# Splitting expert weights and tokens into high and low parts: the low part handed to VectorE later, the weight halves loaded apart

## The chip, the cores and the metric

The kernel runs on one core of one Trainium2 chip. The metric is device time of one launch in microseconds. Before the change it is 754.46 us, the median of three runs (753.71 to 755.72). A difference of about 0.3%, 2.3 us here, is what a measurement of this kernel can tell from none.

## The reference

Attention over 8 batches and 8 heads (512 local positions with a window of 32 and 32 global ones, head size 64) makes 4352 tokens of 512 numbers. They go to 8 experts of 544 places each: the largest (token, expert) logits are taken first. Each expert is a feed-forward layer.

```
logits = x @ w_gate                       # x: 4352 x 512, w_gate: 512 x 8
order = np.argsort(-flat)
for idx in order:                         # greedy: expert e takes at most cap = 544 tokens
    tok, e = (int(idx) // E, int(idx) % E)
    if assigned[tok] >= 0 or counts[e] >= cap:
        continue
    assigned[tok] = e
for e in range(E):
    h = np.maximum(x[mask] @ w1[e], 0.0)  # w1[e]: 512 x 1024
    out[mask] = h @ w2[e]                 # w2[e]: 1024 x 512
```

## The kernel before

**Two stages.** The attention, its gate and the first search for an expert fill the first 278 us of the trace. The change does not touch them. Then `experts` runs eight rounds, `ffn(0)` to `ffn(7)`, one expert each.

**A round.** Products are made in a reduced float format, so each operand is split in a high part (`w1h`, `w2h`, `xh`, `hh`: a copy by ACT that rounds) and a low part (`w1l`, `w2l`, `xl`, `hl`: what is left, a subtraction on DVE). Each product is three matmuls: high by high, high by low, low by high. The first layer (L874) has 8 blocks `f` of 128 columns, each in two halves of 272 tokens; a half is 12 matmuls over the four row blocks `d` of w1, and for `d` = 2 it reads `w1h2` and `w1l2`. ACT then writes `hh` by a Relu (L876) and, after the second half, `h32` (L878); DVE writes `hl`. Then come 64 small matmuls for the last 32 tokens (L889), and 96 matmuls of the second layer (L899), 24 for each of four token tiles. A round of w1 splits has eight pieces: four with columns 0 to 511 (in the code `a`, needed from `f` = 0) and four with columns 512 to 1023 (`b`, needed from `f` = 4).

**Routing beside it.** `Routing.phase` finds the next expert and its tokens by eight search steps. Each is a chain: DVE makes `r_G`, PE multiplies it (`R<-r_oh,r_G`), DVE makes `r_ce`, PE multiplies (`R<-r_ce,big`), DVE scans (`r_pm`) and makes the next `r_G`. From the last step comes `widx` (where the next expert's weights lie), then `r_ohl`, 34 small matmuls `R<-r_ohl,rhs`, the matmuls `R<-c,r_w`, and from them `idx` (where its tokens lie). GpSimd then gathers five tiles of tokens `xg`, PE turns them (L742), ACT writes `xh` (L744) and DVE `xl`.

**What sets the order.** The code writes each engine's instructions in a fixed order, by a plan. `V.now` is the plan's clock, moved on by `step(ns)` after each matmul; `V.busy` is when DVE would be done by estimated durations, whatever DVE waits for. `todo` holds jobs with a tag, a time and a condition; `step` issues one that is due, then as much routing as the plan's clock allows. `calm()` holds splits back while DVE has 200 ns of work ahead. `force(tag)` issues what is left of a tag at once: `force(f"b{ph}")` stands before `f` = 4, `force(f"w{ph}")` (w2) before the small matmuls. `at` puts a job in `todo`. In `split`, ACT's copy is followed at once by DVE's subtraction (L718 to L720), so DVE's next instructions stand behind one that waits for ACT. `load_w1` and `load_w2` gather the two halves (1 MB each) back to back on GpSimd's queue.

Of the kernel before, what the change touches and what calls it, by code (L numbers as in the profile page):

```python
# [8 lines left out]
F32 = mybir.dt.float32  # L9
# [12 lines left out]
E = 8  # L22
# [351 lines left out]
SLACK = 100  # L374
PACE = 250
RELU = 700
CU = 64
LAND = 1000
CF = 1024
# [304 lines left out]
def experts(ctx, tc, A, xd, ident, rt, out):  # L684
# [21 lines left out]
    def load_w1(ph):  # L706
        raws = []
        for k in range(2):
            raw = st.tile([128, 2, FF], F32, name="w1r", bufs=2)
            gather(raw.rearrange("p a b -> p (a b)"), A["w1"], k * E * 128 * 2 * FF, rt.widx[ph][:, :1])  # L710
            raws.append(raw)
        return raws

    def load_w2(ph):
        for k in range(2):
            gather(w2r[k].rearrange("p a b -> p (a b)"), A["w2"], k * E * 128 * 4 * DM, rt.widx[ph][:, :1])

    def split(hi, lo, raw, eng):  # L718
        nc.scalar.activation(hi, raw, AF.Copy)  # L719
        eng.tensor_tensor(lo, raw, hi, op=ALU.subtract)  # L720

    def split_w1(raws, j, eng):
        q = slice(512 * (j % 2), 512 * (j % 2) + 512)
        split(w1h[j // 2][:, q], w1l[j // 2][:, q], raws[j // 4][:, (j // 2) % 2, q], eng)

    def split_w2(j, eng):
        split(w2h[j], w2l[j], w2r[j // 4][:, j % 4], eng)

    def load_x(ph):
        xg = []  # L730
# [4 lines left out]
            xg.append(g)  # L735
        return xg

    def trans_x(xg, t):
        n = sizes[t]
        p = ps.tile([128, 4, 128], F32, name="H", bufs=4)  # L740
        for d in range(4):
            nc.tensor.transpose(p[:, d, :n], xg[t][:n, 128 * d:128 * d + 128], ident[:n, :n])  # L742
        q = slice(128 * t, 128 * t + n)
        nc.scalar.activation(xh[:, :, q], p[:, :, :n], AF.Copy)  # L744
        V.tensor_tensor(xl[:, :, q], p[:, :, :n], xh[:, :, q], op=ALU.subtract)

    out4 = out.rearrange("n (c d) -> (n c) d", c=4)

# [9 lines left out]
    V = rt.V  # L758
    V.now = V.busy = 0.0
    pool, dma, need = [0.0], [0.0], [0.0]  # L760
    fill, todo, raw1 = [], [], {}
    done, cur, mid, wrote = [False], [0], [-1], [0.0]

    def pool_op(ns, nbytes=0):
        pool[0] = max(pool[0], V.now) + ns
        if nbytes:
            dma[0] = max(dma[0], pool[0] + 1800) + nbytes / 360.0
            return dma[0] + 300
        return pool[0]

    def calm():
        return V.busy < V.now + AHEAD

    def chain():
        for ph in range(1, E):
# [16 lines left out]
    def force(tag, n=9):  # L792
        while pending(tag) and n:
            todo.pop([x[0] for x in todo].index(tag))[3]()
            n -= 1

    def step(ns):
        V.now += ns
        low()
        for i, (tag, t, cond, f) in enumerate(todo):  # L800
            if t <= V.now and (cond is None or cond()):
                todo.pop(i)
                f()
                break
        while not done[0] and V.now >= need[0]:
            v = next(routing, None)
            if v is None:
                done[0] = True
            elif v >= 0:
                need[0] = v  # L810

    def low1(p, j):
        split_w1(raw1[p], j, V)

    def low2(j):
        split_w2(j, V)

    def get_w1(p, half):
        raw1[p] = load_w1(p)
        r = [pool_op(1040, 1 << 20) for _ in range(2)]  # L820
        for i in range(4):
            at(f"a{p}", r[i // 2], lambda j=2 * i: low1(p, j), lambda: (half or mid[0] == p - 1) and calm())
        for i in range(4):
            at(f"b{p}", r[i // 2], lambda j=2 * i + 1: low1(p, j), lambda: mid[0] == p - 1 and calm())

    def get_x(p):
        xg = load_x(p)
        for t in range(5):
            r = pool_op(1040, sizes[t] * 2048)
            at(f"x{p}", r, lambda t=t: trans_x(xg, t), lambda: mid[0] == p - 1)  # L830

    def get_w2(p):
        load_w2(p)
        r = [pool_op(1040, 1 << 20) for _ in range(2)]
        for j in range(8):
            at(f"w{p}", r[j // 4], lambda j=j: low2(j), lambda: cur[0] == p and calm())

    def out_tile(ph, t, p):
        n = sizes[t]
# [14 lines left out]
    def ffn(ph):  # L854
# [53 lines left out]
    heat = ps.tile([128, HF], F32, name="H", bufs=4)  # L908
    for _ in rt.phase(0):
        if raws is None and 0 in rt.widx:  # L910
            raws = load_w1(0)
    xg = load_x(0)
    load_w2(0)
    for _ in range(HEAT):
        nc.tensor.matmul(heat[:, :128], ident, ident, start=True, stop=True)
    raw1[0] = raws
    for _ in rt.setup(slice(0, 34)):
        pass
    for j in range(4):
        split_w1(raws, 2 * j, nc.vector)  # L920
    for t in range(5):
        trans_x(xg, t)
    V.now = V.busy
    for j in range(4):
        at("b0", 0, lambda j=j: low1(0, 2 * j + 1), calm)
# [82 lines left out]
```

## Time and profile before

| what | us |
|---|---|
| median of three runs | 754.46 |
| profiled execution: its own time | 759.57 |
| its span | 757.8 |
| PE busy | 695.0 |
| DVE busy | 505.8 |
| ACT busy | 306.9 |
| GpSimd busy | 159.9 |
| round 1, from its first matmul of layer one to the next round's | 59.92 |
| round 2 | 60.14 |
| round 3 | 60.07 |
| round 4 | 60.77 |
| round 5 | 63.01 |
| round 6 (no search beside it) | 55.13 |

Times in the trace count from the start of the span. A row of a timeline gives the start in us, the duration, engine, line, operation and what it writes and reads; in brackets stands how long the engine was idle before it and what ended that. PE is TensorE's matmuls and PEld its loads of weights. A matmul's duration counts its way through the array, and the next starts before it ends, so the pace of PE is read from the distance of the starts. Nearly all work of DVE is recorded under one line, so one goes by the tiles' names.

### The profile page before, as it was taken

The page shows a single profiled execution, that of the slowest core. Times are in us where ns is not written, and L with a number is a line of the kernel's source. Part 1 is how long each engine was busy: PE and PEld are TensorE (multiplying, and loading weights), DVE is VectorE, ACT ScalarE, POOL GpSimd, SP SyncE. Part 2 cuts the span into 40 slices and gives each one's busy share as a digit, 9 for nine tenths or more (in the row PEclk, how much of TensorE's full clock was granted, in tenths as well). Part 3 has the DMA queues.
Part 4 walks back from the last instruction along what each step waited for, and adds up shares of the span by engine and source line. Part 5 has one row for each costly group of instructions (what it writes and reads, how often), then busy time and mean ns, then how long its engine had stood idle before and what let it go on. Part 6 is the DMA issues. An engine that isn't in the chain of part 4 may idle for free. (4 is left out here: it accounts for less than half of the span.)

```text
span 757.8 us, 21849 instructions
## 1 busy us (share of the span) xinstructions
PE 695.0 (92%) x9012; PEld 569.1 (75%) x9012; DVE 505.8 (67%) x1855; ACT 306.9 (40%) x841; POOL 159.9 (21%) x190
## 2 busy tenths in 40 slices
PE   8999999999995289999999999999999997999993
PEld 6667777777773169879879878878977975988982
DVE  6787877787776778678677776767766865641400
ACT  4656766665751034243143234333324322542310
POOL 5221221221100130330231142033034034312011
PEclk9999999999997569999999999999999999999997
DMA  9998878979701160350171071062063047331000
GB/s 358 410 356 312 320 279 292 325 277 331 279 20 58 41 241 1 124 194 26 53 253 38 6 270 68 6 238 99 2 235 106 2 165 241 106 116 55 2 32 28
DMA packets 32419, 120.56 MB, mean 159 GB/s; under 512 B 6720, under 2 KB 6976, under 8 KB 24128
## 3 DMA queue, kind: packets, MB, share of 16 engines
q1 hardware_dynamic: 22080, 67.78, 24.3%
q0 software_dynamic: 10240, 51.39, 19.1%
q8 instruction: 71, 1.16, 0.6%
q14 instruction: 28, 0.23, 0.1%
HBM read 101.32 MB, written 17.83 MB: 157 GB/s over the span
## 5 line engine op out<-in xcount | busy, mean ns | idle before, releaser
L874 PE MATMUL H<-xh,w1h 128*128 128x272 f32 x512 | 151.9, 297 | 4.3 <-ACT xh L744 4.3
L874 PE MATMUL H<-xh,w1l 128*128 128x272 f32 x512 | 152.4, 298 | 0.0
L874 PE MATMUL H<-xl,w1h 128*128 128x272 f32 x512 | 151.9, 297 | 0.1
L145 ACT ACTIVATE p<-p,nm 128x128 f32<-128x128 f32 x256 | 81.8, 391 | 66.5 <-DVE ls L165 34.3
L876 ACT ACTIVATE hh<-H 128x272 fp32r<-128x272 f32 x128 | 51.0, 398 | 134.4 <-PE H L874 114.0
L899 PE MATMUL Y<-w2h,hh 128*128 128x512 f32 x256 | 103.9, 406 | 0.0
L899 PE MATMUL Y<-w2l,hh 128*128 128x512 f32 x256 | 102.0, 398 | 0.0
L874 PEld LDWEIGHTS H<-xh,w1h 128*128 128x128 f32 x512 | 98.3, 192 | 4.9 <-ACT xh L744 4.4
L899 PE MATMUL Y<-w2h,hl 128*128 128x512 f32 x256 | 101.8, 398 | 0.0
L874 PEld LDWEIGHTS H<-xl,w1h 128*128 128x128 f32 x512 | 98.2, 192 | 1.4 <-DVE xl L406 0.8
L874 PEld LDWEIGHTS H<-xh,w1l 128*128 128x128 f32 x512 | 98.0, 191 | 0.7 <-issue 0.2
L406 DVE TENSOR_TENSOR w2l<-w2r,w2h 128x512 fp32r<-128x512 f32 x64 | 43.9, 690 | 48.4 <-ACT w2h L719 47.9
L134 PE MATMUL S<-qk,qz 128*64 128x128 f32 x1024 | 70.8, 279 | 5.5 <-DVE qz L86 2.4
L86 POOL COPY qz<-q 64x544 f32<-64x544 f32 x60 | 38.3, 639 | 151.7 <-DMA q<-in_qk_dram 106.6
L134 PEld LDWEIGHTS S<-qk,qz 128*64 128x64 f32 x1024 | 55.0, 137 | 18.4 <-issue 11.3
L406 DVE SCALAR_TENSOR_TENSOR hl<-H,hh 128x272 fp32r<-128x272 f32 x128 | 54.5, 435 | 20.3 <-ACT h L878 10.7
L141 DVE CUSTOM_DVE_ANT_0 p<-S,mask 128x128 f32<-128x128 f32 x256 | 58.7, 285 | 6.2 <-PE S L134 5.1
L847 ACT ACTIVATE y<-Y 128x512 f32<-128x512 f32 x32 | 19.1, 598 | 103.0 <-PE Y L899 79.5
L719 ACT ACTIVATE w1h<-w1r 128x512 fp32r<-128x512 f32 x64 | 36.9, 624 | 55.7 <-DVE r_c L406 29.8
L406 DVE TENSOR_TENSOR w1l<-w1r,w1h 128x512 fp32r<-128x512 f32 x60 | 40.9, 686 | 26.5 <-ACT w1h L719 24.6
L899 PEld LDWEIGHTS Y<-w2h,hh 128*128 128x128 f32 x256 | 48.1, 188 | 11.4 <-issue 2.0
L899 PEld LDWEIGHTS Y<-w2h,hl 128*128 128x128 f32 x256 | 48.1, 188 | 11.1 <-issue 0.8
(166 smaller groups left out, 1169.3 us busy)
## 6 DMA issues: line engine op xcount, KB each, us to landing
vw<-in_vw_dram SPq DMA_DIRECT2D x32, 1040.0 KB, 8.1
qk<-in_qk_dram SPq DMA_DIRECT2D x32, 432.0 KB, 5.6
q<-in_qk_dram SPq DMA_DIRECT2D x32, 272.0 KB, 6.1
xd<-xs SPq DMA_DIRECT2D x8, 1024.0 KB, 6.7
xd<-xg SPq DMA_DIRECT2D x64, 8.0 KB, 6.0
xg<-xd,idx POOLq DMA_INDIRECT x40
mask<-in_mask_dram SPq DMA_DIRECT2D x1, 512.0 KB, 4.9
cf<-in_cf_dram SPq DMA_DIRECT2D x1, 512.0 KB, 12.5
```

The lines of the kernel that those rows point to most:

```text
L86: eng.tensor_copy(z[r, :, h, :], q[r].rearrange("p (j i) -> p j i", i=32))
L134: nc.tensor.matmul(st[64 * r:64 * r + 64, c, :], z[:, j].rearrange("p h i -> p (h i)"), kw[:, k0:k0 + 128], start=True, stop=True)
L141: nc.vector.tensor_tensor_reduce(s.p[:, c, :], st[:, c, :], mask[:, 4 * s.u + c, :], 1.0, -BIG, ALU.add, ALU.max, nm[:, c:c + 1])
L145: nc.scalar.activation(s.p[:, c, :], s.p[:, c, :], AF.Exp, bias=nm[:, c:c + 1], scale=SCALE)
L406: return op(*args, **kw)
L719: nc.scalar.activation(hi, raw, AF.Copy)
L847: nc.scalar.activation(y[:n], p[:n], AF.Copy)
L874: nc.tensor.matmul(p, w[d][:, fs], x[:, d, q], start=(d + k == 0), stop=(d + k == 5))
L876: nc.scalar.activation(hh[:, f, q], p, AF.Relu)
L899: nc.tensor.matmul(p, h[:, f, q], w[f], start=(f + k == 0), stop=(f + k == 9))
```

## The change

`split` issues ACT's copy alone. With `late` set, DVE's subtraction goes into a list `lag` with a time: `SPLIT` = 850 ns later on the plan's clock for weights, 1290 ns for tokens (`SPLIT + 4 * 110`). `settle` issues what is due in each `step`; `settle(True)` issues all that is left, at the end of `force` (for all tags but `out`) and at a round's end. `calm` also holds splits back while two are in `lag`. Only the first round's first splits stay as they were. The second half of w1 and of w2 is gathered by a job of its own, `APART` = 3000 ns of the plan after the first; the `b` pieces wait until both halves are loaded and the `a` pieces issued.

```
+SPLIT = 850
+APART = 3000
...
-    def split(hi, lo, raw, eng):
+    def split(hi, lo, raw, late, ns=SPLIT):
         nc.scalar.activation(hi, raw, AF.Copy)
-        eng.tensor_tensor(lo, raw, hi, op=ALU.subtract)
+
+        def rest():
+            V.tensor_tensor(lo, raw, hi, op=ALU.subtract)
+        if late:
+            lag.append((V.now + ns, rest))
+        else:
+            rest()
...
-        nc.scalar.activation(xh[:, :, q], p[:, :, :n], AF.Copy)
-        V.tensor_tensor(xl[:, :, q], p[:, :, :n], xh[:, :, q], op=ALU.subtract)
+        split(xh[:, :, q], xl[:, :, q], p[:, :, :n], late, SPLIT + 4 * 110)
...
     def calm():
-        return V.busy < V.now + AHEAD
+        return V.busy < V.now + AHEAD and len(lag) < 2
...
     def force(tag, n=9):
...
+        if tag != "out":
+            settle(True)
+
+    def settle(all=False):
+        while lag and (all or lag[0][0] <= V.now):
+            lag.pop(0)[1]()

     def step(ns):
         V.now += ns
         low()
+        settle()
...
     def get_w1(p, half):
-        raw1[p] = load_w1(p)
-        r = [pool_op(1040, 1 << 20) for _ in range(2)]
-        for i in range(4):
-            at(f"a{p}", r[i // 2], lambda j=2 * i: low1(p, j), lambda: (half or mid[0] == p - 1) and calm())
-        for i in range(4):
-            at(f"b{p}", r[i // 2], lambda j=2 * i + 1: low1(p, j), lambda: mid[0] == p - 1 and calm())
+        raw1[p] = []
+
+        def go(k):
+            raw1[p].append(load_w1(p, k))
+            r = pool_op(1040, 1 << 20)
+            for j in (4 * k, 4 * k + 2):
+                at(f"a{p}", r, lambda j=j: low1(p, j), lambda: (half or mid[0] == p - 1) and calm())
+            for j in (4 * k + 1, 4 * k + 3):
+                at(f"b{p}", r, lambda j=j: low1(p, j),
+                   lambda: mid[0] == p - 1 and not pending(f"a{p}", f"g{p}") and calm())
+        go(0)
+        at(f"g{p}", V.now + APART, lambda: go(1))
...
             out_tile(ph, t, p)
         while nxt < E and (pending(f"g{nxt}", f"h{nxt}", f"a{nxt}", f"x{nxt}", f"v{nxt}") or nxt not in raw1):
             step(120)
+        settle(True)
```

`get_w2` is cut in two by a `go(k)` of its own in the same way, and line numbers of the experts' code grow by up to 21.

**ACT, the pieces of w1 for round 3.** Before, in the second layer of round 2, ACT has the last pieces `w1h1`, `w1h2`, `w1h3` (columns 512 to 1023) ahead of the tokens `xh`; `y` is a finished output tile:

```order
L847 ACTIVATE y_7685<-Y_7586 128x512
L719 ACTIVATE w1h1_4822<-w1r_7509 128x512
L719 ACTIVATE w1h2_4823<-w1r_7511 128x512
L719 ACTIVATE w1h3_4824<-w1r_7511 128x512
L744 ACTIVATE xh_4847<-H_7723 128x4x128
L744 ACTIVATE xh_4847<-H_7734 128x4x128
```

Now, in layer one of round 3, the last two of them stand between block `f` = 3 (`hh` twice and `h32`) and block `f` = 4 (the last two `hh`):

```order
L895 ACTIVATE hh_4849<-H_7947 128x272
L895 ACTIVATE hh_4849<-H_7969 128x272
L897 ACTIVATE h32_4851<-H_7969 128x32
L717 ACTIVATE w1h2_4823<-w1r_7537 128x512
L717 ACTIVATE w1h3_4824<-w1r_7537 128x512
L895 ACTIVATE hh_4849<-H_8013 128x272
L895 ACTIVATE hh_4849<-H_8033 128x272
```

Two pieces moved past `xh` and half of the next round's layer one, to the place where `force` empties the `b` list; rounds 1 to 5 all have this, rounds 0, 6 and 7 have the pieces earlier.

**DVE, between round 2 and round 3.** Before, the tokens' low parts `xl` (four tiles of 128 and one of 32) are done ahead of the first `r_ce` of the new search:

```order
L406 TENSOR_TENSOR xl<-H,xh 128x4x128 x2
L406 TENSOR_TENSOR r_G<-r_hi,cf 128x544
L406 TENSOR_TENSOR xl<-H,xh 128x4x128 x2
L406 SCALAR_TENSOR_TENSOR r_mo<-r_asgv,r_mv 128x34
L406 TENSOR_TENSOR r_oh<-r_v,r_mo 128x272
L406 TENSOR_TENSOR xl<-H,xh 128x4x32
```

Now three of the five stand behind it:

```order
L408 TENSOR_TENSOR r_oh<-r_v,r_mo 128x272
L408 TENSOR_TENSOR xl<-H,xh 128x4x128 x2
L408 TENSOR_SCALAR r_lo<-r_u 128x34
L408 TENSOR_SCALAR r_lof<-r_lo 128x34
L408 TENSOR_TENSOR r_ce<-R,dk 128x256
L408 TENSOR_TENSOR xl<-H,xh 128x4x128 x2
L408 TENSOR_TENSOR xl<-H,xh 128x4x32
```

What moved is `r_ce`, which reads the result of PE's matmuls `R<-r_oh,r_G`: on PE that group now stands ahead of the last tile's four transposes, where it stood 20 matmuls into layer one. So it is for the turns from rounds 0, 1, 2, 3 and 4 to the next.

**DVE, the four `r_ohl` in the second layer of round 2.** Before, each stands behind a low part of w1; now two are free of it:

```order
L406 TENSOR_TENSOR rhs<-r_ohh,ids 128x306 x2
L406 TENSOR_TENSOR w1l_4825<-w1r,w1h_4821 128x512
L406 TENSOR_TENSOR r_ohl<-r_hb,tab 128x544
L406 TENSOR_TENSOR w1l_4826<-w1r,w1h_4822 128x512
L406 TENSOR_TENSOR r_ohl<-r_hb,tab 128x544
```

```order
L408 TENSOR_TENSOR rhs<-r_ohh,ids 128x306 x2
L408 TENSOR_TENSOR r_ohl<-r_hb,tab 128x544 x2
L408 TENSOR_TENSOR w1l_4825<-w1r,w1h_4821 128x512
L408 TENSOR_TENSOR r_ohl<-r_hb,tab 128x544
L408 TENSOR_TENSOR w1l_4826<-w1r,w1h_4822 128x512
L408 TENSOR_TENSOR r_ohl<-r_hb,tab 128x544
```

On PE the matmuls `R<-r_ohl,rhs` stand after 63 of the 96 matmuls of layer two in rounds 0 to 5 (before after 57 in round 0, 63 in round 1, 62 in rounds 2 to 5), and `R<-c,r_w`, which give `idx`, after 72 (round 5: 70), where they stood after 66, 72, 71, 71, 71 and 69. On GpSimd's queue the halves now go w1, w2, an output tile, w1, w2, an output tile, then the five `xg`; before w1, w1, w2, w2, an output tile, `xg`.

More of the change, by code (lines that the diff above doesn't have):

```diff
@@ L704, in gather, with load_w1, load_w2, split_w1 @@
                                      in_offset=bass.IndirectOffsetOnAxis(ap=idx, axis=0))
[L706 to L716, printed above, removed]
-    def split(hi, lo, raw, eng):
-        nc.scalar.activation(hi, raw, AF.Copy)
-        eng.tensor_tensor(lo, raw, hi, op=ALU.subtract)
-    def split_w1(raws, j, eng):
+    def load_w1(ph, k):
+        raw = st.tile([128, 2, FF], F32, name="w1r", bufs=2)
+        gather(raw.rearrange("p a b -> p (a b)"), A["w1"], k * E * 128 * 2 * FF, rt.widx[ph][:, :1])
+        return raw
+    def load_w2(ph, k):
+        gather(w2r[k].rearrange("p a b -> p (a b)"), A["w2"], k * E * 128 * 4 * DM, rt.widx[ph][:, :1])
+    def split(hi, lo, raw, late, ns=SPLIT):
+        nc.scalar.activation(hi, raw, AF.Copy)
+        def rest():
[4 more added lines that the diff above has]
+            rest()
+    def split_w1(raws, j, late):
         q = slice(512 * (j % 2), 512 * (j % 2) + 512)
-        split(w1h[j // 2][:, q], w1l[j // 2][:, q], raws[j // 4][:, (j // 2) % 2, q], eng)
-    def split_w2(j, eng):
-        split(w2h[j], w2l[j], w2r[j // 4][:, j % 4], eng)
+        split(w1h[j // 2][:, q], w1l[j // 2][:, q], raws[j // 4][:, (j // 2) % 2, q], late)
+    def split_w2(j):
+        split(w2h[j], w2l[j], w2r[j // 4][:, j % 4], True)
     def load_x(ph):
@@ L736, in load_x, with trans_x @@
         return xg
-    def trans_x(xg, t):
+    def trans_x(xg, t, late):
         n = sizes[t]
@@ L760, in experts @@
     pool, dma, need = [0.0], [0.0], [0.0]
-    fill, todo, raw1 = [], [], {}
+    fill, lag, todo, raw1 = [], [], [], {}
     done, cur, mid, wrote = [False], [0], [-1], [0.0]
@@ L812, in low1 @@
     def low1(p, j):
-        split_w1(raw1[p], j, V)
+        split_w1(raw1[p], j, True)
     def low2(j):
-        split_w2(j, V)
+        split_w2(j)
     def get_w1(p, half):
-        raw1[p] = load_w1(p)
-        r = [pool_op(1040, 1 << 20) for _ in range(2)]
-        for i in range(4):
-            at(f"a{p}", r[i // 2], lambda j=2 * i: low1(p, j), lambda: (half or mid[0] == p - 1) and calm())
-        for i in range(4):
-            at(f"b{p}", r[i // 2], lambda j=2 * i + 1: low1(p, j), lambda: mid[0] == p - 1 and calm())
+        raw1[p] = []
[9 more added lines that the diff above has]
+        at(f"g{p}", V.now + APART, lambda: go(1))
     def get_x(p):
@@ L829, in get_x, with go @@
             r = pool_op(1040, sizes[t] * 2048)
-            at(f"x{p}", r, lambda t=t: trans_x(xg, t), lambda: mid[0] == p - 1)
+            at(f"x{p}", r, lambda t=t: trans_x(xg, t, True), lambda: mid[0] == p - 1)
     def get_w2(p):
[L833 to L836, printed above, removed]
+        def go(k):
+            load_w2(p, k)
+            r = pool_op(1040, 1 << 20)
+            for j in range(4 * k, 4 * k + 4):
+                at(f"w{p}", r, lambda j=j: low2(j), lambda: cur[0] == p and calm())
+        go(0)
+        at(f"v{p}", V.now + APART, lambda: go(1))
     def out_tile(ph, t, p):
@@ L910, in experts @@
         if raws is None and 0 in rt.widx:
-            raws = load_w1(0)
+            raws = [load_w1(0, k) for k in range(2)]
     xg = load_x(0)
-    load_w2(0)
+    for k in range(2):
+        load_w2(0, k)
     for _ in range(HEAT):
@@ L919, in experts @@
     for j in range(4):
-        split_w1(raws, 2 * j, nc.vector)
+        split_w1(raws, 2 * j, False)
     for t in range(5):
-        trans_x(xg, t)
+        trans_x(xg, t, False)
     V.now = V.busy
```

## The prediction

> **What bounds the kernel now.** I read the view by stage first, a window for each round from its first matmul of layer one to the next round's (rounds 1 to 4 whole, round 5 in pieces). The columns are busy us of PE, PEld, DVE, ACT and GpSimd, then the granted clock, the DMA share and GB/s.
>
> ```profile
> 338.25:398.17 59.92, 58.24 (x574) 49.27 (x572) 43.03 (x118) 20.80 (x51) 14.04 (x14) 1.00 0.30 108
> 398.17:458.31 60.14, 58.04 (x573) 49.17 (x571) 42.82 (x118) 20.73 (x51) 14.23 (x14) 1.00 0.31 107
> 458.31:518.38 60.07, 58.12 (x574) 49.19 (x572) 42.64 (x118) 20.73 (x51) 14.75 (x14) 1.00 0.31 108
> 518.38:579.15 60.77, 58.12 (x574) 49.15 (x572) 42.57 (x118) 20.77 (x51) 14.70 (x14) 1.00 0.31 108
> 635.00:641.00 6.00, 2.67 (x18) 1.89 (x16) 1.32 (x4) 0.60 (x1) 4.20 (x5) 0.97 0.68 221
> 641.00:647.00 6.00, 4.71 (x19) 4.41 (x20) 2.83 (x7) 2.67 (x6) 0.00 (x0) 0.50 0.70 268
> ```
>
> PE is busy 58 of 60 us in a round, DVE 43. So the order of PE's matmuls is the time, and the change can win or lose only where PE waits inside it. What it takes from DVE's idle time is far more than PE can get back. The view of waits over 338 to 635 us shows both sides (us in total, times, longest):
>
> ```profile
> DVE w2l L406 <- ACT w2h L719: 24.7, 27, 1.4
> DVE w1l L406 <- ACT w1h L719: 16.6, 14, 3.0
> PEld L473 <- DVE r_ohl L406: 4.6, 5, 1.4
> PEld L473 <- DVE r_G L406: 3.8, 14, 0.5
> ```
>
> DVE stands 24.7 + 16.6 = 41.3 us waiting for ACT's high parts; of that PE feels at most 4.6 + 3.8 = 8.4 us, by the routing's products. How one of these waits reaches PE is seen in the chain of waits, read over round 5:
>
> ```profile
> 586.51 0.19 ACT h L878
> 586.70 0.53 ACT w2h L719
> 587.25 0.69 DVE w2l L406
> 587.94 0.15 DVE r_x L406
> 588.09 0.34 DVE r_ce L406
> 588.47 0.27 PE R L473 x2
> ```
>
> ACT's copy, the subtraction behind it, then the routing's small `r_ce` that stood behind the subtraction, then PE.
>
> The last two windows above are a hole of another kind: between 635 and 641 us PE is busy 2.67 of 6 us and then runs 6 us at clock 0.50. That costs 3.3 us idle and up to 3.0 by the clock. The profiled execution's own time is 759.57 us, 5.1 above the median of 754.46, and nothing else in it is that large. I take the hole as belonging to that execution, not to the timed runs.
>
> **The sum, part by part.**
>
> *The low parts leave DVE's way (gain).* Three places in a round show it on PE:
>
> ```profile
> 587.88 0.29 PE L874 MATMUL H<-xh,w1h 128*128 128x272 f32 x1
> 588.47 0.27 PE L473 MATMUL R<-r_ce,big 128*128 128x128 f16 x2 [0.30 <-DVE r_ce L406]
> 564.39 0.39 PE L899 MATMUL Y<-w2h,hh 128*128 128x512 f32 x1
> 564.62 0.39 PE L899 MATMUL Y<-w2l,hh 128*128 128x512 f32 x1
> 566.03 1.25 PE L473 MATMUL R<-r_ohl,rhs 128*32 128x64 bf16 x34 [1.02 <-DVE r_ohl L406]
> ```
>
> The first pair is 0.59 us apart where 0.13 is the pace, so 0.46 is lost. In the second place 564.62 + 0.39 = 565.01 is the end of the last matmul and 566.03 the next start: 1.0 lost, the worst of the five (4.6 in five times is 0.9 in the mean as PEld sees it, and PEld is early by some of that). With a third one by `r_G` of 0.3 a round loses 1.1 to 1.7 us. Five rounds make 5.5 to 8.5. In the new order the subtraction stands where ACT's copy is long done, and two of the four `r_ohl` come ahead of any low part. The plan counts DVE's own durations, so what stays is small. I take 6.0 us, bounds 3.0 and 8.4.
>
> *Two pieces of w1 forced ahead of block 4 (cost).* This wait is not in the trace, but each link of it is. ACT does `w1h2` and `w1h3` only after the Relu of block 3, which waits for the block's last matmul; the two subtractions follow at once, since `force` ends in `settle(True)`, so here nothing is handed over late. The links, from rounds 5 and 6:
>
> ```profile
> 597.43 0.29 PE L874 MATMUL H<-xh,w1l 128*128 128x272 f32 x1
> 597.55 0.29 PE L874 MATMUL H<-xh,w1h 128*128 128x272 f32 x1
> ...
> 597.75 0.40 ACT L876 ACTIVATE hh<-H 128x272 fp32r<-128x272 f32 x1 [0.73 <-PE H L874]
> 598.05 0.19 ACT L878 ACTIVATE h<-H 128x32 f32<-128x32 f32 x1
> 598.12 0.63 ACT L719 ACTIVATE w2h<-w2r 128x512 fp32r<-128x512 f32 x1
> ...
> 586.58 1.15 ACT L719 ACTIVATE w2h<-w2r 128x512 fp32r<-128x512 f32 x2
> ...
> 653.19 1.33 DVE L406 TENSOR_TENSOR w2l<-w2r,w2h 128x512 fp32r<-128x512 f32 x2
> ```
>
> Let S be the start of the block's last matmul (597.43). The Relu starts at S + 0.32, a copy at S + 0.69; one copy ends at S + 1.32, two at S + 1.84 (1.15 for a pair). DVE starts some 0.04 after the first copy: one subtraction ends near S + 2.05, two near S + 2.69 (1.33 for a pair). PE goes on at 0.125 a matmul: its 7th (first use of `w1h2`) would be at S + 0.88 and can be at 1.35 (0.47 lost); the 9th (`w1l2`) would then be at 1.60 and can be at 2.08 (0.48 lost); the 12th (`w1l3`) would be at 2.45 and can be at 2.72 (0.27 lost). Together 1.2 us, in rounds 1 to 5: 6.0 us. Bounds: the first two alone, 0.95 a round, and 1.5 if a link is slower; 4.8 to 7.5. Nothing covers it: PE has no other work in the order, and DVE's `hl` and scan behind the subtractions have slack only because PE stands too.
>
> *The turn between two rounds (cost).* `r_ce` now stands ahead of the third token tile's low part, and waits for PE's `R<-r_oh,r_G`, which waits for the fourth tile's transposes. In the turn from round 4 to 5 before:
>
> ```profile
> 569.41 0.20 PE L473 MATMUL R<-c,r_w 128*128 128x5 bf16 x2
> ...
> 575.37 0.60 PE L742 MATMUL H<-ident,xg 128*128 128x128 f32 x4
> 575.73 0.48 PE L899 MATMUL Y<-w2l,hh 128*128 128x512 f32 x1
> ...
> 578.01 1.21 PE L742 MATMUL H<-ident,xg 128*128 128x128 f32 x8 [0.79 <-DMA xg<-xd,idx]
> 579.15 0.40 PE L874 MATMUL H<-xh,w1h 128*128 128x272 f32 x1
> 579.38 0.29 PE L874 MATMUL H<-xl,w1h 128*128 128x272 f32 x1
> ...
> 581.72 0.29 PE L874 MATMUL H<-xl,w1h 128*128 128x272 f32 x1
> 581.94 0.28 PE L473 MATMUL R<-r_oh,r_G 128*32 128x16 f16 x17
> 582.06 0.17 PE L473 MATMUL R<-rem,one 128*32 128x16 f16 x1
> 582.16 0.39 PE L874 MATMUL H<-xh,w1l 128*128 128x272 f32 x1
> ...
> 582.30 0.42 DVE L406 TENSOR_TENSOR r_ce<-R,dk 128x256 f16<-128x256 f32 x1 [0.15 <-PE R L473]
> ```
>
> The fourth tile's transposes wait for its tokens until 578.01, 8.6 us after `R<-c,r_w` made the indices; the first matmul that reads `xl` comes 1.37 later. Now it comes later than that: four transposes 0.36 (575.37 to 575.73), the group to its last start 0.22 (581.72 to 582.06, less a matmul's pace), to `r_ce` 0.24 (582.06 to 582.30), `r_ce` 0.34 (the chain's row), one `xl` 0.69 (as the `w2l` of the chain, of the same size), a start 0.06, in all 1.91, so 0.54 more. The group itself leaves layer one, where it took 582.16 - 581.72 - 0.125 = 0.31, so 0.23 net. To that comes what `R<-c,r_w` stands later in PE's order, 0.23 us a matmul of layer two (564.39 to 564.62), since the tokens follow it at a fixed distance: six matmuls in the turn from round 0 (1.4), none from round 1, one (0.23) from rounds 2, 3, 4 and 5. The turns from rounds 0 to 4 cost 1.63, 0.23, 0.46, 0.46 and 0.46, the one from round 5, which has no such group, 0.23: 3.5 us, bounds 2.0 (a part hides where PE waits for tokens anyway) and 5.5.
>
> *The halves apart.* The second half of w1 now queues behind the first of w2 and an output tile, and all begin later, since the search ends some 7 matmuls of layer two (1.6 us) later. ACT's `y` copies stand behind the pieces that wait for it. PE needs them two tiles of layer two (11 us) later, and the pieces by the next round, so I count nothing. Without that cover it would be 2.8 us a round, the time of one half (2^20 bytes) at the 379 GB/s of the stretch in which weights come in:
>
> ```profile
> 560.00:568.00 8.00, 6.98 (x59) 5.40 (x58) 5.83 (x15) 3.31 (x6) 0.62 (x1) 1.00 0.97 379
> ```
>
> The sum on the profiled execution: 759.57 - 6.0 + 6.0 + 3.5 = 763.1 with the hole; without it, as in the timed runs, 754.46 + 3.5 = **758.0 us**, 0.5% slower.
>
> One rule could make it worse. A stretch at half clock follows the hole (641 to 647, clock 0.50), while round 4, with its wait of 1.02 us, has 1.00 throughout. The Trainium skill, "TensorE: Matmul & The Clock Gate" (Part 1, the HAM clock gate, and "A second HAM failure mode"), says that an idle window of about 3.4 us halves the clock, and that short idles between groups of matmuls, if frequent, can do so too. By the second rule each wait at block 4 could cost such a stretch; round 4's row speaks against it, and no run here yet shows a wait at every round's block 4.
>
> **The rivals.**
>
> *The two sides cancel.* The gain is at its upper bound 8.4 and the cost at its lower, 4.8 + 2.0: 754.46 - 8.4 + 6.8 = 752.9; with the middle of both nearer, 754 to 756. For it speaks that the plan's estimates of DVE are long (180 ns + 1.05 ns an element is 718 ns for a subtraction of 512; a pair above takes 1330), so that the search's products meet results that lie ready; against it that the two costs are chains of fixed links. Chance 0.24.
>
> *The hole goes, and it was in every run.* If the stretch of 635 to 641 us belongs to each execution (tokens that share the DMA engines with weights) and the new order of gathers ends it, 6.3 us go: 754.46 - 6.3 + 3.5 = 751.7. For it: DMA share 0.68 and 221 GB/s in the window. Against it: the tokens' place behind both halves of both weights stays, and the median is already 5.1 us below the execution that has it. It decides for faster only if the rest costs less than 4.0. Chance 0.13.
>
> *The waits at block 4 bring the clock down.* Five stretches of 6 us at half speed cost 3 each: 758.0 + 15 = 773.0. Chance 0.03.
>
> **How the numbers follow.** The forecast (slower by 2.3 to 8.5 us) has 0.60. Faster by over 0.3% (below 752.2) gets 0.13, within 0.3% (about what a measurement of this kernel can tell from no change) 0.24, slower (above 756.7) 0.60 + 0.03 = 0.63. The range is 752.0 to 763.0: below, it takes in the cancelling case and stops just above the middle of the hole's rival; above, both costs at their upper bounds (7.5 + 5.5) with a gain of 4.5 give 754.46 + 8.5 = 763.0. Outside lie the clock's case, half of the hole's, and all bounds bad at once.
>
> **What would show it.** Right: in rounds 1 to 5 a wait of PE on `w1h` and `w1l`, about 1.2 us in sum, half-way through layer one (from its 97th matmul on); a wait on `xl` of 0.5 to 0.8 at each turn from rounds 0 to 4; the waits on `r_ohl` and `r_G` down from 8.4 to 2 or 3; DVE's waits for ACT down from 41 us to under 15; rounds 1 to 4 at 60.2 to 61.2 us. Wrong: rounds of 59.5 or less, which would mean that the copies come earlier than behind block 3's Relu, or that PE was kept by the routing at that point anyway; or the waits at block 4 there and the total lower, which would leave a gain that I have not seen.

## The result, and the profile after

The changed kernel takes 763.38 us (median of six runs, 759.9 to 767.46) where the kernel before took 754.47 in the same set: a ratio of 1.0127, 95% interval 1.0085 to 1.017. It is slower by 8.9 us; 3.5 were forecast. Two later sets put the same pair at 1.0073 (1.0043 to 1.0103) and 1.0029 (0.9999 to 1.006), by medians 4.2 and 4.9 us. The last ratio leaves out three of the changed kernel's twelve executions (768.31 to 774.1 us) as slow; the median of the other nine is 763.38 us, 3.8 above the kernel before. What differs between the sets is the kernel before: 754.47, 759.74, 758.87, 759.58, 753.3 and 759.55 us. The changed kernel had 763.38, 763.91 and 764.49. So between sets the same kernel moves by up to 0.8%, and the 0.3% that a measurement can tell from none holds at best within a set. The later sets ran on the chips numbered 0, 7, 10, 7 and 0; chip 7 gave both 758.87 and 753.3, so the chip alone does not explain it.

The view by stage of the changed kernel, in rounds from 1 to 6 (columns as in the prediction; the seventh is the granted clock):

```profile
339.69:400.92 61.23, 59.64 (x573) 50.87 (x571) 41.75 (x117) 20.35 (x50) 14.13 (x14) 0.97 0.29 106
400.92:463.63 62.71, 59.95 (x574) 50.61 (x572) 42.98 (x119) 20.58 (x51) 14.79 (x14) 0.97 0.30 104
463.63:523.89 60.26, 58.47 (x574) 49.38 (x572) 43.12 (x119) 20.47 (x51) 13.82 (x14) 1.00 0.31 108
523.89:585.06 61.17, 58.58 (x573) 49.35 (x572) 43.02 (x119) 20.60 (x51) 14.74 (x14) 1.00 0.31 106
585.06:646.52 61.46, 59.54 (x557) 50.50 (x555) 41.28 (x115) 20.16 (x51) 13.89 (x14) 0.97 0.31 106
646.52:699.50 52.98, 52.65 (x410) 46.99 (x410) 23.89 (x48) 22.20 (x54) 14.13 (x14) 1.00 0.34 122
```

Three things stand out. Rounds 1 to 4 are 0.2 to 2.6 us longer than before. In three of the five rounds with a search the mean clock is 0.97 where it was 1.00 (0.99 in round 5). And rounds 5 and 6 together are 114.4 us where they were 118.1: the hole is gone. The view of waits, 339 to 646 us:

```profile
DVE w1l L408 <- ACT w1h L717: 11.7, 14, 1.1
PEld H L746 <- DMA xg<-xd,idx: 9.9, 13, 1.3
PEld H L893 <- ACT w1h L717: 3.0, 5, 0.6
PEld H L893 <- DVE xl L408: 2.7, 4, 0.7
PEld H L893 <- DVE w1l L408: 2.1, 5, 0.4
```

PE's waits on `r_ohl` and `r_G`, 8.4 us before, have left the list, and DVE's waits for ACT's high parts of the weights fell from 41.3 to 11.7. In their place stand five waits at block 4 (on `w1h` and `w1l`) and four on `xl`. Here is one of each kind in two timelines, at block 4 of round 2 and at the turn into that round:

```profile
417.59 0.29 PE L893 MATMUL H<-xh,w1l 128*128 128x272 f32 x1
418.26 0.39 PE L893 MATMUL H<-xh,w1h 128*128 128x272 f32 x1 [0.38 <-ACT w1h L717]
418.49 0.29 PE L893 MATMUL H<-xl,w1h 128*128 128x272 f32 x1
418.99 0.39 PE L893 MATMUL H<-xh,w1l 128*128 128x272 f32 x1 [0.21 <-DVE w1l L408]
```

```profile
398.13 0.66 PE L746 MATMUL H<-ident,xg 128*128 128x128 f32 x4
399.76 0.66 PE L746 MATMUL H<-ident,xg 128*128 128x128 f32 x4 [0.98 <-DMA xg<-xd,idx]
400.35 0.28 PE L475 MATMUL R<-r_oh,r_G 128*32 128x16 f16 x17
...
400.92 0.39 PE L893 MATMUL H<-xh,w1h 128*128 128x272 f32 x1
401.79 0.60 PE L893 MATMUL H<-xl,w1h 128*128 128x272 f32 x1 [0.47 <-DVE xl L408]
402.18 0.43 PE L893 MATMUL H<-xh,w1l 128*128 128x272 f32 x1
402.40 0.43 PE L893 MATMUL H<-xh,w1h 128*128 128x272 f32 x1
```

At block 4 two starts lie 0.67 and 0.50 us apart where the pace is 0.125. At the turn, TensorE waits 1 us for tokens and some 0.63 us on `xl` (the first two starts of the round are 0.87 us apart, 0.23 in the kernel before), and from 401.79 on the matmuls last 0.43 us and more where they last 0.29 elsewhere. That is the clock, as windows over the same places show:

```profile
398.01:401.42 3.41, 2.26 (x32) 1.53 (x31) 1.97 (x6) 2.28 (x5) 1.50 (x2) 1.00 0.54 173
401.42:404.83 3.41, 3.04 (x13) 3.00 (x13) 1.11 (x3) 0.14 (x1) 0.98 (x1) 0.50 0.20 77
417.50:421.00 3.50, 2.91 (x22) 2.42 (x21) 2.72 (x6) 1.63 (x5) 0.00 (x0) 1.00 0.02 5
```

In the window that spans the turn PE is busy 2.26 of 3.41 us; the next has a clock of 0.50. At block 4, with its waits, the clock stays at 1.00. Between 290 and 730 us this profile has three such half-clock stretches of 3.41 us, all at turns.

### The profile page after: what moved, and what is told of

It is laid out like the page before. It is cut to its first block, busy times and chain, and to the rows that moved or that the text cites. A ratio compares the mean times of both kernels' runs of the same rounds, so it can differ in the third digit from the quotient of the medians.

```text
span 760.2 us, 21827 instructions
## 1 busy us (share of the span) xinstructions
PE 698.3 (92%) x9012; PEld 571.8 (75%) x9012; DVE 506.1 (67%) x1855; ACT 305.6 (40%) x841; POOL 159.6 (21%) x190
## 5 line engine op out<-in xcount | busy, mean ns | idle before, releaser
L893 PE MATMUL H<-xh,w1h 128*128 128x272 f32 x512 | 154.3, 301 | 1.9 <-ACT w1h L717 1.9
L893 PE MATMUL H<-xl,w1h 128*128 128x272 f32 x512 | 153.9, 301 | 2.2 <-DVE xl L408 2.2
L918 PEld LDWEIGHTS Y<-w2l,hh 128*128 128x128 f32 x256 | 48.2, 188 | 9.7
L408 DVE TENSOR_TENSOR w1l<-w1r,w1h 128x512 fp32r<-128x512 f32 x64 | 42.9, 687 | 18.4 <-ACT w1h L717 18.2
L408 DVE TENSOR_TENSOR w2l<-w2r,w2h 128x512 fp32r<-128x512 f32 x64 | 41.9, 685 | 16.2 <-ACT w2h L717 15.4
```

What stands on the lines that cost most here:

```text
L408: return op(*args, **kw)
L893: nc.tensor.matmul(p, w[d][:, fs], x[:, d, q], start=(d + k == 0), stop=(d + k == 5))
L918: nc.tensor.matmul(p, h[:, f, q], w[f], start=(f + k == 0), stop=(f + k == 9))
```

## The experiments

Each set is timed side by side with the kernel before. The theory that the expectations call A is the one just read from the profile.

**The changed kernel again.**

> The changed kernel once more, for a second profile. Theory A (1.2 us of wait ahead of block 4 in five rounds, 0.7 us of wait on xl at the turns, and the idle pieces of a turn together bring the granted clock to one half for a window of 3.4 us at some turns, 1.5 us each): 760 to 767, with windows of half clock at two to five of the seven turns and not at the same ones as in the profile after, and none around block 4. Theory B (the loss is the weights that arrive later since their two halves are loaded apart): the same time, no window of half clock beyond those of the first profile needed. Theory C (the waits of block 4 bring the clock down): windows of half clock that begin within 5 us behind block 4.

763.91 us, 1.0073 (1.0043 to 1.0103). The profile has half-clock stretches at all five turns from rounds 0 to 4, one of them 6.83 us long, none behind block 4. Theory C falls. The places differ from the first profile's, as A says.

**The forced pieces half a block earlier.**

```
-                force(f"b{ph}")          # ahead of both halves of block 4
+                if f == 3 and hf:        # ahead of block 3's second half
+                    force(f"b{ph}")
```

> The changed kernel with the two forced pieces of w1 issued half a block earlier, between the two halves of block 3; all else stands nearly as in the changed kernel. Theory A: the first half of block 4 goes from 2.8 us to 1.6 in rounds 1 to 5, some 1.0 to 1.2 us each, so 5 to 6 us less than the changed kernel: 757 to 759; the windows of half clock at the turns stay. Theory B: the weights arrive as late as in the changed kernel, so the wait stays and the time too, within 1.5 us. Theory C: 6 us of waits less and the windows gone as well, 4 us more: 752 to 754.

757.96 us, 0.9976 (0.9951 to 1.0): 5.95 us under the changed kernel by the medians. The first half of block 4 takes 1.52 us in each of rounds 1 to 5, where the changed kernel has 2.8 to 2.9. Some 0.2 us of the difference is the routing group on `r_ce`, which the changed kernel has in this half and this one in block 4's second half; the waits cost about 1.15 us a round. In this timeline of round 2 the starts go on at their pace at block 4's 7th matmul (416.28) and its 9th (416.53), the two that waited in the changed kernel (418.26 and 418.99):

```profile
416.15 0.29 PE L894 MATMUL H<-xh,w1l 128*128 128x272 f32 x1
416.28 0.29 PE L894 MATMUL H<-xh,w1h 128*128 128x272 f32 x1
416.40 0.29 PE L894 MATMUL H<-xl,w1h 128*128 128x272 f32 x1
416.53 0.29 PE L894 MATMUL H<-xh,w1l 128*128 128x272 f32 x1
```

The stretches at the turns stay (four). So the term of 6.0 us for block 4 is right (five times 1.15 is 5.8), and the clock falls at the turns without these waits.

**The tokens' low parts at once.**

```
+        nc.scalar.activation(xh[:, :, q], p[:, :, :n], AF.Copy)
+        nc.vector.tensor_tensor(xl[:, :, q], p[:, :, :n], xh[:, :, q], op=ALU.subtract)
+        lag.append((V.now + SPLIT + 4 * 110, paid))   # paid() only adds to V.busy
```

> The changed kernel, but the tokens' low parts are issued straight behind their high parts, while the planner's clocks are charged as if they still came late, so that TensorE's and ScalarE's orders stay word for word and on VectorE only the five subtractions of a turn stand earlier. Theory A: the wait on xl of 0.7 us goes at turns 0 to 4 (3.5 us less), and with it some of the crowd of idle pieces at the turn, so half or all of the half-clock windows (2 to 6 us less); given back up to 1.5 us where r_oh and r_G come later for the transposes of the turn: 754 to 759. Theory B: no change, within 1.5 us. Theory C: 3.5 us less at most and the windows stay: 759 to 761.

761.67 us, 1.0025 (0.9998 to 1.0051): 2.2 us under the changed kernel, less than the 5 to 10 that A expected. The wait on `xl` went, but `r_oh` then came late for the same turn, and the clock fell as before (three stretches):

```profile
398.65 0.66 PE L746 MATMUL H<-ident,xg 128*128 128x128 f32 x4 [0.71 <-DMA xg<-xd,idx]
399.94 0.28 PE L475 MATMUL R<-r_oh,r_G 128*32 128x16 f16 x17 [0.64 <-DVE r_oh L408]
...
400.51 0.60 PE L901 MATMUL H<-xh,w1h 128*128 128x272 f32 x1
401.12 0.59 PE L901 MATMUL H<-xl,w1h 128*128 128x272 f32 x1
```

A wait was exchanged for another one 2 us earlier; that `xl` alone crowds the turn is wrong.

**Both edits.**

> Both of these edits of the changed kernel together: forced pieces of w1 half a block earlier, and the tokens' low parts issued at once. Theory A: the two add up, 8 to 11 us less than the changed kernel: 751 to 755, with no window of half clock at the turns, so as fast as the kernel before or up to 3 us faster. Theory B: within 1.5 us of the changed kernel. Theory C: 752 to 756 as well, so this run tells A and C apart only by where the clock falls.

754.39 us, 0.9929 (0.9899 to 0.9958): 9.5 us under the changed kernel, as A expected, and faster than the kernel before of this set (759.74). But three stretches of half clock are still there, at turns; that part of the expectation missed.

**The kernel before again.**

> The kernel before, unchanged, for a second profile of it: does the hole of 7 us that its first profile shows at 635 to 647 come again, and does the clock fall at its turns? If the hole belongs to the one execution, there is none or it is elsewhere. Theory A (idle pieces that crowd at a turn take the clock down for 3.4 us): the kernel before has one wait of 1.0 us for tokens at a turn and none on xl, so zero to two windows of half clock at its turns. The time is that of the kernel before, within 0.3%.

758.59 us, 0.9992 (0.9964 to 1.0019). The hole is there again, smaller:

```profile
636.00:642.00 6.00, 3.42 (x23) 2.67 (x22) 1.77 (x4) 1.08 (x2) 3.44 (x4) 0.97 0.72 259
642.00:648.00 6.00, 5.28 (x49) 4.20 (x49) 3.03 (x8) 1.57 (x4) 0.01 (x1) 0.50 0.51 195
```

So it does not belong to one execution. No other turn of this profile has half clock.

**Matmuls that fill the idle time of the turn.**

```
+STIR = (0, 0, 3, 4, 0)
+        for d in range(STIR[t] if late else 0):
+            nc.tensor.matmul(p[:, d], ident, ident, start=True, stop=True)
```

> The changed kernel with seven matmuls of 128 by 128 per turn that feed nothing (into the buffer that the transposes then fill), three ahead of the third tile's transposes and four ahead of the fourth's, where TensorE waits for tokens: about 0.21 us each, 1.5 us of a turn's 2.1 to 2.6 us of idle time, and no other instruction moves. Theory A (it is the crowd of idle pieces that brings the clock down): the windows of half clock at the turns go, all or nearly all, so 3 to 6 us less than the changed kernel, less up to 0.4 us a turn where the tokens had already come: 1 to 5 us less. A rival, D (the clock falls at the turns on a beat of its own, or from heat, whatever TensorE does there): the windows stay, and the time is the changed kernel's or up to 3 us more.

762.02 us, 1.0049 (1.0018 to 1.0079): 1.9 us under the changed kernel by the medians, with overlapping intervals. The clock is the plain result. One stretch is left, at the turn from round 0; the other turns have none:

```profile
398.30:401.71 3.41, 2.94 (x43) 2.50 (x41) 2.07 (x6) 1.92 (x4) 1.11 (x2) 1.00 0.41 150
401.71:405.12 3.41, 3.41 (x28) 3.35 (x29) 2.05 (x5) 0.47 (x2) 0.99 (x1) 1.00 0.22 82
```

PE is busy 2.94 of 3.41 us at the turn, and the next window keeps the full clock. The order is the changed kernel's but for the fillers, so the idle time of the turn is what brings the clock down, and theory D falls. The gain in time is less clear: rounds 1 to 4 take 245.3 us here with one stretch and 245.4 in the first profile of the changed kernel with two. Where the fillers had no idle time to fill they cost: round 6 takes 54.4 us in place of 53.0.

**The lag alone.** Halves loaded together, second-column pieces (`b`) free as before:

```
-                   lambda: mid[0] == p - 1 and not pending(f"a{p}", f"g{p}") and calm())
+                   lambda: mid[0] == p - 1 and calm())
-        at(f"g{p}", V.now + APART, lambda: go(1))
+        go(1)
-        at(f"v{p}", V.now + APART, lambda: go(1))
+        go(1)
```

> One part of the change alone: the low parts handed over late, but the two halves of w1 and w2 loaded together, and a piece of w1's second columns free to go as soon as VectorE is calm, as before. Nearly all pieces of w1 are split ahead of the round's first matmul, and the tokens' transposes stand 8 to 20 matmuls earlier in the turn. Theory A: no wait at block 4, at most 0.3 us on xl, one token wait at a turn or none, so no more windows than the kernel before has; the gain of the low parts out of VectorE's way stays: 3 to 8 us less than the kernel before. Theory E (handing the low parts over late is what costs, since each low part then ends later): 2 to 6 us more than the kernel before.

753.1 us, 0.9905 (0.9868 to 0.9943): 7.2 us under the kernel before by the ratio (5.8 by the medians), as A has it; theory E falls. PE's order shows a part of where that comes from. These are the places in the second layer of round 2 (out of its 96 matmuls) at which PE has the matmuls `R<-c,r_w`, behind which the tokens can be asked for, and the transposes of the five token tiles:

```
kernel                               R<-c,r_w   transposes
before                                  71      90 94 96 96 96
changed                                 72      92 95 96 96 96
lag alone                               56      75 79 83 88 89
halves apart alone                      68      87 91 95 96 96
changed, second columns free            54      73 77 81 86 87
```

With the lag alone the search ends 15 matmuls earlier in this round, 3.5 us at 0.23 each, so that all transposes lie among matmuls of layer two and none waits at the end. In rounds 1, 3, 4 and 5 it ends 7 to 10 matmuls earlier, in round 0 six later. By the profiles the larger part of the gain is the hole, which is gone here. Rounds 1 to 4 take 237.9 us where they took 240.9, round 0 takes 63.6 for 60.5 (with 6.83 us of half clock behind the turn from it), and rounds 5 and 6 take 110.6 for 118.1. These are the two last, first before, then with the lag alone:

```profile
579.15:642.16 63.01, 57.89 (x575) 49.23 (x573) 40.54 (x116) 19.94 (x50) 16.88 (x17) 0.99 0.35 123
642.16:697.29 55.13, 55.00 (x409) 49.00 (x409) 22.59 (x47) 20.85 (x52) 12.40 (x12) 0.95 0.29 101
580.18:638.57 58.39, 57.32 (x556) 48.70 (x555) 41.79 (x116) 21.77 (x52) 14.21 (x15) 1.00 0.32 112
638.57:690.80 52.23, 52.23 (x410) 46.79 (x408) 21.78 (x45) 20.80 (x51) 15.45 (x15) 1.00 0.37 129
```

**Both edits and the fillers.**

> The combination of the run before (forced pieces of w1 half a block earlier, the tokens' low parts at once) with the seven idle-filling matmuls per turn. Theory A: the three windows of half clock that the combination still had at its turns go too, 2 to 4 us less than the combination alone, which stood 0.7% under the kernel before: 1.0 to 1.3% under it. D: the windows stay, 0.4 to 0.7% under it.

754.96 us, 0.995 (0.9919 to 0.9981). One stretch of half clock is left, at the turn from round 0, but the time is no lower than without fillers: rounds 1 to 5 are 2.6 us shorter (297.8 for 300.4), while rounds 0 and 6 are 2.9 longer (117.5 for 114.6). A's gain was there and was paid back, as far as one profile of each can tell: round 0 alone varies by 2.9 us between executions of the changed kernel.

**The rule or the halves?** The changed kernel has a rule with its halves: no second-column piece goes until all first-column pieces have gone. The two come apart in the next two kernels; the first keeps the rule and loads the halves together (the two `go(1)` lines above), the second keeps the halves apart and drops the rule (the `lambda` line above).

> The changed kernel with the two halves of w1 and of w2 loaded together, as before; the changed rule stays, by which a second-column piece of w1 may go only when all first-column pieces have gone. Theory F (two costs that come with the halves apart: pieces that arrive too late for block 4, 5 to 6 us; and the rule, which takes second-column pieces out of the turn into layer one, so that routing and with it the tokens come later and idle pieces crowd at the turn, 5 to 8 us): the order still has the transposes at the very end of layer two, so the wait at block 4 goes and the turns stay as in the changed kernel, with windows of half clock: 5 to 7 us less than the changed kernel, within 0.4% of the kernel before. Theory B (the halves apart are the whole loss): as fast as the run with the lag alone, 0.9% under the kernel before.

759.26 us, 0.9981 (0.9958 to 1.0005). No wait at block 4 (1.70 us in each round), and half clock at the same five turns, as F says. So with the lag and the rule, loading the halves apart does cost: 1.0073 in the changed kernel against 0.9981 here, in two sets whose kernels before agree (759.74 and 759.58).

> The changed kernel with the two halves still loaded apart, but the old rule: a second-column piece may go as soon as VectorE is calm. Two pieces are still forced ahead of block 4, while the tokens' transposes stand some 20 matmuls earlier in the turn. Theory F: block 4 still waits 1.0 to 1.2 us in rounds 1 to 5, the turns are calm, with at most one window of half clock: 6 to 9 us less than the changed kernel, 0 to 0.6% under the kernel before. Theory B: the changed kernel's time, 0.7% over the kernel before or more.

751.52 us, 0.9903 (0.9866 to 0.994): as fast as the lag alone, and faster than F expected, since block 4 waits less than in the changed kernel (its first half takes 1.92 to 2.50 us, and 1.92 is what the lag alone has without a wait) and the hole is gone (rounds 5 and 6: 110.6 us). At the turn from round 2 PE has no idle time to speak of (the changed kernel's window above, at the turn from round 1, had 2.26 of 3.41):

```profile
451.60:455.00 3.40, 3.36 (x22) 2.85 (x22) 2.41 (x5) 1.67 (x3) 2.72 (x3) 1.00 0.64 195
455.00:458.40 3.40, 3.40 (x36) 2.55 (x36) 1.84 (x6) 1.47 (x3) 0.87 (x2) 1.00 0.28 99
458.40:461.80 3.40, 3.19 (x36) 2.47 (x35) 2.00 (x5) 1.55 (x4) 0.83 (x2) 1.00 0.21 80
```

Not every turn is as calm. The turn from round 0 has 6.83 us of half clock behind it, and at the turns from rounds 1 and 3 PE waits 1.2 us for `r_G`, in windows busy 2.2 of 3.41 us behind which the clock stays up. Theory B, which blamed the halves, falls with this run. The rule is what costs, and the halves apart cost only together with it.

**The halves apart alone, with the rule.**

```
-        if late:
+        if False:                                       # no low part is handed over late
-        return V.busy < V.now + AHEAD and len(lag) < 2
+        return V.busy < V.now + AHEAD
```

> The other part of the change alone: the halves of w1 and w2 loaded apart, with the changed rule, but each low part handed to VectorE straight behind its high part, as before. Theory F: the transposes stand late here too (8 to 12 matmuls later than before), so 0 to 1.0% over the kernel before, from waits at block 4 (0.3 to 1.0 us a round, W1.2 and W1.3 stand half a block earlier than in the changed kernel) and at the turns. If the loss came from the lag and the halves together only, this kernel is within 0.2% of the kernel before.

758.57 us, 0.9986 (0.9966 to 1.0006): no slower, a little below what F expected. It has block 4's waits (its first half takes 2.2 to 3.2 us, where the kernel before has 1.5 to 2.25), but no wait on `xl` over 0.5, no half clock at any turn (though a window from 574.33, ahead of the turn from round 4, is busy only 1.87 of 3.41 us), and no hole. Its time hides two sides: rounds 1 to 4 take 243.5 us, 3 more than before, and rounds 5 and 6 take 113.3 for 118.1.

**The lag alone, tokens at once.**

> The run with the lag alone, but the tokens' low parts issued at once (the planner charged as if late, so that the orders of TensorE and ScalarE stay). A version meant to beat both kernels. In the run with the lag alone the round's first routing matmul waited 1.1 to 1.35 us in four of seven rounds, since VectorE has three subtractions of tokens ahead of r_pm and r_G; here one of the three is left there. Theory A: 0.7 to 1.0 us less in each of these rounds, 2 to 4 us under the lag alone, 1.2 to 1.5% under the kernel before. Against it: r_oh stands behind two subtractions that wait for ScalarE, and what is won at r_G is lost at r_oh: within 0.3% of the lag alone.

754.27 us, 0.9934 (0.9905 to 0.9962): not better than the lag alone. PE waited 0.6 to 1.5 us for `r_ce` at four turns, and still 0.65 to 0.8 us for `r_G`; the alternative in the expectation holds.

**The lag from round 1 on.** Round 0 of the changed kernel is longer than before in two of its three profiles (62.3 and 63.4 us against 60.5), with the search ending six matmuls later.

```
-        if late:
+        if late and cur[0]:
```

> The changed kernel, but in round 0 the low parts go straight behind their high parts, as before; the lag begins with round 1, from where the order is the changed kernel's word for word. In round 0 the matmuls on c and r_w stand behind 60 matmuls of layer two in place of 72, so the first tokens are asked for 2.8 us earlier and four of five transposes lie among layer two's matmuls. Theory G (the first turn's 2.5 to 3.6 us come from the lag's delay of routing in round 0): round 0 goes from 62 to 63 us back to 59.8 to 60.5, 2.5 to 3.5 us less than the changed kernel: 0.3 to 0.5% less. Rival H (the tokens of the first turn come late for a reason in the DMA queues, whatever round 0's order): round 0 stays at 62 or more, within 0.15% of the changed kernel.

760.39 us, 1.0082 (1.0047 to 1.0116), in a set where the kernel before is at 753.3. Round 0 takes 61.9 us. That is neither of the two values expected, and it settles nothing: a third profile of the changed kernel, taken below, has 60.5 in round 0 with the same code.

> The halves apart with the old rule (second-column pieces free as soon as VectorE is calm), and the lag from round 1 on. A version meant to beat both kernels. Theory G: 2.5 to 3 us less than the same kernel with the lag in round 0, so 1.2 to 1.4% under the kernel before. H: 0.9 to 1.0% under it.

752.3 us, 0.9968 (0.9939 to 0.9998); round 0 takes 60.67 us. Its own time does not beat the same kernel with the lag in round 0 (751.52), though the kernel before was 6 us faster in this set, so the two ratios can't be set side by side. The first turn stays open.

**The pair once more.**

> The kernel before, unchanged, for a third profile. Theory J (the hole of turn 5 and its window of half clock come in some executions and are what takes 754 us to 759): an execution of 758 to 760 us has the hole and a window of half clock of 6.8 us at 640; one of 752 to 755 has neither, and its last round takes 53 us in place of 55 to 56. If an execution of 752 to 755 has the hole too, J falls, and the 5 us come from elsewhere in the program, perhaps from ahead of the experts.

761.57 us, 1.0016 (0.9987 to 1.0046). The profiled execution took 762.69 and has the hole:

```profile
641.00:647.00 6.00, 1.55 (x10) 0.97 (x9) 2.01 (x5) 1.62 (x4) 2.65 (x3) 0.67 0.78 283
```

All three profiles of the kernel before have it, but all three are of executions of 758 to 763 us. Whether one of 753 has it wasn't seen, so J is neither shown nor refuted. This profile also has half clock from 567.95 and, at the turn from round 4, from 581.61: the kernel before can lose the clock there too. What makes the hole was not tested, but GpSimd's queue shows a candidate. In these three profiles it issues both halves of the next w1 2.5 and 3.8 us behind the last gather of tokens, ahead of the round's first matmul (636.88 and 638.16 behind 634.39 in the first profile). In the other 15 profiles, none of which has the hole, the first of them comes 6.2 us or more behind, after the round has begun. That these weights hold up the tokens is argued, not shown.

> The changed kernel, unchanged, in the same set: 760 to 766 us as in both sets before. If the kernel before is at 754 here, the distance is 1.1 to 1.3%, if it is at 759, 0.6 to 0.8%: it is the kernel before that has two times, not the changed one. The profile shows windows of half clock at two to five turns and 1.2 us of wait at block 4 in rounds 1 to 5.

764.49 us, 1.0029 (0.9999 to 1.006), with half clock at five turns, and block 4's first half at 2.8 to 2.9 us in rounds 1 to 5.

Set side by side, the ratios to the kernel before are:

| | second columns free | second columns behind the first (rule) |
|---|---|---|
| lag, halves together | 0.9905 | 0.9981 |
| lag, halves apart | 0.9903 | 1.0127, 1.0073, 1.0029 (the change) |
| no lag | 1 (before, halves together) | 0.9986 (halves apart) |

The two versions in the first column beat both kernels in their sets, where the kernel before took 758.87 and 759.58 us. Their own 753.1 and 751.52 us are level, to 0.4%, with the 753 to 754 that it takes in two other sets, and the one such version timed there (with the lag from round 1 on) gains 0.3%. So the change is two parts of which one is worth -0.95% alone and the other, with its rule, nothing alone, and together they are +0.3 to +1.3%; how much of the -0.95% is only the hole depends on whether the faster executions of the kernel before have it.

## Why the prediction was wrong

The direction was right, and the size was 3.5 where 8.9 was measured. The step that failed is the turn: its 3.5 us end with the waits and put the clock at nothing there, where the runs showed three to seven stretches of half clock, 4.5 to 10 us by the estimate below. A second step, that the hole belongs to one execution, left out a gain. Where the sum comes close, to the 4.2 and 4.9 us of the later sets, two errors of opposite sign make up for each other, and that is luck. By its own steps:

*The low parts leave DVE's way, -6.0.* The waits on which it rests went as it said, and further: 8.4 to nothing that the view lists, DVE's waits 41.3 to 11.7 (under 15 was forecast). The 6.0 us themselves were not measured apart. Alone the lag is worth 7.2 us, but most of that comes by ways that the step did not have: the end of the hole, and an earlier end of the search, which the changed kernel does not get.

*Two pieces ahead of block 4, +6.0.* Right in place, kind and size: about 1.15 us in each of rounds 1 to 5, 0.55 and 0.37 of it at the first two links (the third shows no wait of its own, since the routing group on `r_ce` stands ahead of it), and 5.95 us came back when the pieces stood half a block earlier.

*The turn, +3.5.* The wait on `xl` came as forecast (0.5 to 0.8 expected, 0.61 to 0.63 at four turns). What failed is that the sum stops there. The clock has no term in it; the prediction gave it to a rival at block 4, with a chance of 0.03. It came at the turns. Rounds 1 to 4 of the three profiles of the changed kernel take 245.4, 249.4 and 251.9 us, with two, five and six times 3.41 us at half clock in them; two of the three profiles before have 240.4 and 240.9 with none, the third 243.7 with one. A line through the changed kernel's three points has a slope of some 1.5 us for each stretch of 3.41 us, and without the clock leaves 242.2 us, 1.5 above the kernel before. The sum has 1.6 for these rounds: the gain and block 4 cancel, and the turns from rounds 1 to 4 are 0.23 and three times 0.46. So the three terms hold together, as far as three points can show it, and three to seven such stretches (over all turns of a profile), 4.5 to 10 us by that slope, came on top.

The sentence of the Trainium skill that the prediction weighed, in "TensorE: Matmul & The Clock Gate" (section "A second HAM failure mode"), that short and frequent idles make the clock fall too, is borne out by these traces: in 18 profiles the clock fell 45 times between 290 and 730 us, each time behind a 3.41 us window in which PE was busy at most 2.36 us, and never behind a busier one. Such a window does not suffice: 14 as idle as that had no fall, one of them, 1.86 us busy, at the turn from round 2 in the first profile of the changed kernel. The waits at block 4, 0.55 and 0.37 us, were not enough in any of them; but a turn has one or two waits for tokens, each about 1 us, one on `xl`, and the starts between them. The fillers showed it: 2.94 us busy, and no fall.

*The hole belongs to that execution.* Wrong for the executions that can be seen: it is in all three profiles of the kernel before and in none of the changed kernel, which has 3 us less in rounds 5 and 6, with a wait at block 4 and a stretch of half clock in them; the lag alone, without these two, has 7.5 us less. This is a gain that the sum lacks, and it hides a part of the loss. The rival that had the hole in every run and saw it go fits these profiles, and had the sign of the whole wrong.

*The halves apart, 0.* This is where the order went wrong, though the sum counted its waits elsewhere. The step looked at the loads, and by themselves they lose nothing: with the rule dropped they may be apart. With the rule kept they bring the waits at block 4, which the sum has in a term of its own. The rule that came with them (`not pending(...)` in the diff) pushes the second-column pieces behind the turn, into layer one, and the search's end in round 2 from matmul 54 to 72. The prediction compared 72 with 71, the place before, and saw one matmul. It did not ask what the lag alone would have done, and so did not see the gain that the rule takes away: 1.3 to 2.2% between the two kernels that differ in that one line (the changed kernel's three ratios against 0.9903), 0.8% with the halves together.

What stays open: the first turn (60.5 to 63.4 us for round 0 with the same code), what makes the hole, what besides an idle window decides that the clock falls, and why the kernel before takes 753 to 754 us in two sets and 759 to 760 in four.

## What to carry to other kernels

When a change has several parts, price each part alone and in pairs against the order that it produces, not only the whole against the order before: a condition on one queue can take away what another part wins. Idle pieces of an engine with a clock gate should be added up over a window, here 3.41 us, before each is called small; here the waits of one turn brought the clock down, and the smaller ones at block 4 did not. An anomaly in the one profiled execution is better profiled twice before it is left out of a sum. And compare two kernels round by round: here a gain in rounds 5 and 6 hid a loss in rounds 1 to 4.

## What the runs showed of the hardware

The clock's stretches in the records come in multiples of 3.413 us, on one grid through an execution: in the second profile of the changed kernel they begin at 342.61, 404.05 and 465.49, eighteen such steps apart. A round of about 61 us therefore meets the grid at almost the same phase each time, which may be why in one execution five turns lose the clock and in another three; that the phase decides is argued here, not shown.
